# Rounding the token and channel weights to float32 during attention, by way of a DRAM scratch

## The chip, the cores and the metric

The kernel runs on one core of one Trainium2 chip. The metric is the device time of one execution in microseconds. Each kernel is run several times, and the median is compared. Engines are named as in the profile: PE multiplies matrices, PEld loads its stationary operand, DVE is the vector engine, ACT the scalar engine, POOL the GpSimd engine, SP the engine that issues every DMA of this kernel.

## The reference

Three layers follow each other for 4 batches of 768 tokens and 384 channels. First comes a gated linear recurrence over 8 heads of 48 channels ("attention" below). Then comes a layer that mixes tokens by a spatial matrix under a gate. Last come two dense layers over tokens (768 to 256 to 768) and two over channels (384 to 1536 to 384), each pair with a residual:

```python
state = f[:, :, t, :, None] * state + np.einsum('bhd,bhe->bhde', k[:, :, t], v[:, :, t])
y[:, :, t] = np.einsum('bhd,bhde->bhe', q[:, :, t], state)
...
h = np.maximum(x @ w_in, 0.0)                      # u and v are the halves of h
v_s = np.einsum('ts,bsd->btd', w_spatial, v_n) + b_spatial[None, :, None]
x = (u * v_s) @ w_out
...
h = np.maximum(xt @ w_tok1, 0.0) @ w_tok2
u = x + h.transpose(0, 2, 1)
return u + np.maximum(u @ w_ch1, 0.0) @ w_ch2
```

The matrices w_in, w_out, w_tok1, w_tok2, w_ch1 and w_ch2 arrive as float64, w_spatial as float32.

## The kernel before, in words

Every matrix product is done three times: each operand is a sum of a high and a low part (`h` and `l`), and the product of both low parts is left out (`mm3`, lines 126 to 132). So each weight must be split before PE can use it. `split_weight` (line 57) does this in pieces of 128 rows and up to 384 columns. A float64 piece goes through these steps: SP loads it as pairs of 32-bit words (L72). DVE puts the high word's bits in place with two instructions (L78, L81). ACT scales the low word (L85). POOL adds it (L86). ACT squares the high word (L87). DVE sets values to zero that are too small for float32 (L91). These instructions are called the rounding. After it, ACT copies the piece into the high part (L92), and POOL or DVE subtracts to get the low part (L101). A float32 piece needs only a load (L96), the copy and the subtraction. The pool `wst` holds three pieces in flight (`bufs` is 3), with one tile for the loaded words and one, `wsa`, for the result.

The token and channel weights are 34 pieces: w_t1 has 6 pieces of 256 columns, w_t2 has 4, w_c1 12 (8 named wc1, 4 named wc1x) and w_c2 12 of 384 columns.

Work is written down as lists of steps, which `weave` mixes with each other. A scheduler then sets the final order on each engine from these lists. Each engine runs its instructions strictly in that order. In the first phase, for each batch, come the normalised input layer (`s1`: products pv and pu), the token mixing (`mix`: products ps, then DVE L439, ACT L443, DVE L440 and L444) and the output product (`out1`: px, which goes to the DRAM scratch x1d). The attention of the batch after it is woven in; one unit is two heads over half of the tokens. A unit needs on DVE two scans and a product (L204, L211, L214), state updates (L254, L267) and a subtraction (L358). After the third batch's turn there is no attention left to weave in. There the fourth batch's products, the token layers of the first batch (p with wt1, wt2) and the start of the channel layers (p with wc1, po with wc2) are woven with the splitting of the token and channel weights:

```python
        weave(rest + s1(B - 1, 0) + s1(B - 1, 1), staged(st_a + st_b))
...
        m, rest = s23(B - 1)
        weave(m, conv)
...
        weave(c2(0), st_c[:12])
```

This stretch, from about 372 to 520 us, is called the transition below. What follows it is channel layers (L602, L603, L615) for all batches.

Of the kernel before, what the change touches and what calls it, by code (L numbers as in the profile page):

```python
# [18 lines left out]
def tile_kernel(ctx, tc, fkqs, v, w_in, w_sp, b_sp, w_out, w_t1, w_t2, w_c1, w_c2, out):  # L19
    nc = tc.nc  # L20
# [22 lines left out]
    def f32(ap):  # L43
        return ap.bitcast(F32)
# [8 lines left out]

    # weights as sums of two parts of 12 bits each; float64 is rounded to float32 on the way
    LEAST = 3.4332275390625e-05 ** 2

    def split_weight(pool, stage, src, name, n, cols, eng, first=0, order=None):
        """Tiles of both parts, and the steps that fill them, piece by piece."""
        wide = src.dtype == mybir.dt.uint64
        h = pool.tile([P, n, cols], F32R, name=name + "h")  # L60
        l = pool.tile([P, n, cols], F32R, name=name + "l")
        if wide:
            src = src.bitcast(U32)
        srcr = src.rearrange("(n p) c -> n p c", p=P)

        def piece(i, c0, width):
            sl = (slice(None), i, slice(c0, c0 + width))
            at = stage.tile([P, WST], U32, tag="wsa", name=f"{name}sa{i}{c0}")
            a = at[:, :width]
            if wide:  # L70
                st = stage.tile([P, WST, 2], U32, tag="wst", name=f"{name}st{i}{c0}")
                nc.sync.dma_start(  # L72
                    out=st[:, :width, :].rearrange("p c t -> p (c t)"),
                    in_=srcr[first + i][:, 2 * c0 : 2 * (c0 + width)],
                )
                yield
                lo, hi = st[:, :width, 0], st[:, :width, 1]
                nc.vector.tensor_scalar(  # L78
                    out=a, in0=hi, scalar1=3, scalar2=0x3FFFFFFF, op0=ALU.logical_shift_left, op1=ALU.bitwise_and
                )  # L80
                nc.vector.scalar_tensor_tensor(  # L81
                    out=a, in0=hi, scalar=0xC0000000, in1=a, op0=ALU.bitwise_and, op1=ALU.bitwise_or
                )
                # the low word's first 3 bits, rounded
                nc.scalar.activation(lo, lo, AF.Copy, scale=2.0**-29)  # L85
                nc.gpsimd.tensor_tensor(out=a, in0=a, in1=lo, op=ALU.add)  # L86
                nc.scalar.activation(f32(hi), f32(hi), AF.Square)  # L87
                yield
                # zero below float32's least normal number
                a = f32(a)  # L90
                nc.vector.scalar_tensor_tensor(out=a, in0=f32(hi), scalar=LEAST, in1=a, op0=ALU.is_ge, op1=ALU.mult)  # L91
                nc.scalar.copy(h[sl], a)  # L92
                yield
            else:
                a = f32(a)
                nc.sync.dma_start(out=a, in_=srcr[first + i][:, c0 : c0 + width])  # L96
                yield
                nc.scalar.copy(h[sl], a)
                yield
                yield  # L100
            eng.tensor_tensor(out=l[sl], in0=a, in1=f32(h[sl]), op=ALU.subtract)  # L101

        where = [(i, c0, min(WST, cols - c0)) for i in range(n) for c0 in range(0, cols, WST)]
        return h, l, [partial(piece, *x) for x in (order(where) if order else where)]

    def staged(pieces):
        """Steps in which each piece is one stage behind the one after it."""
        gens = []

        def step(n):  # L110
            if n < len(pieces):
                gens.append(pieces[n]())
            for g in gens[max(0, n - 3) : n + 1]:
                next(g, None)

        return [partial(step, n) for n in range(len(pieces) + 3)]

    def weave(main, *fillers):
        """Emit the steps of main with those of the others spread evenly before them."""
        for n, m in enumerate(main):  # L120
            for fl in fillers:
                for x in fl[len(fl) * n // len(main) : len(fl) * (n + 1) // len(main)]:
                    x()
            m()

    def mm3(ps, pairs, first=True, **kw):
        """ps += sum over (lh, ll, rh, rl) of (lh + ll)^T (rh + rl) without the product of both low parts."""
        n = len(pairs)
# [5 lines left out]
    def body(general):  # L134
        # ---------------- phase 1 pools
        x1d = dram.tile([B, S, DM], F32, name=f"x1d{int(general)}")
# [58 lines left out]
        def chunked(u, b, hf, p, fs, fkq, vt):  # L195
            ki, qi = fkq[:, 1, :], fkq[:, 2, :]
            n0 = hf * NCW
            # decay from the chunk's start, and its inverse (from the chunk's end backwards); both scans pass
            # through all chunks and start anew where the factor is zero and the other operand is not
            pg = at2.tile([P, 2, W], F32, tag="pg", name=f"pg{u}")  # L200
# [14 lines left out]
            yield  # L215
            # keys with tokens on partitions
            ncs = NCW if hf == 0 else NCW - 1
# [111 lines left out]
        def att_unit(b, hf, p):  # L329
            """The steps of one pair of heads over half of the tokens."""  # L330
            u = f"{b}{hf}{p}"
# [33 lines left out]
        def att(units):  # L365
            """Steps of these units in turn, the first of each ahead of the unit before it."""
            gens = [att_unit(*x) for x in units]
# [95 lines left out]

        # ---------------- phase 1
        winh, winl, steps = split_weight(
# [10 lines left out]
        out_steps = staged(st_b)  # L476
        rest = []
        for b in range(B - 1):
            if b:
                weave(s1(b, 0), rest)  # L480
            a, rest = s1(b, 1), []
            m, rest = s23(b)
            steps = att(half(b + 1, 0) + half(b + 1, 1))
            cut = len(steps) * len(a) // len(a + m)
            weave(a, steps[:cut], out_steps)
            weave(m, steps[cut:])
            out_steps = []
        right.close()
        wr2 = ExitStack()
        w2p = wr2.enter_context(tc.tile_pool(name="w2p", bufs=1, side="right"))  # L490
        t1h, t1l, st_a = split_weight(w2p, wst, w_t1, "wt1", NCH, DT, nc.gpsimd)
        t2h, t2l, st_b = split_weight(w2p, wst, w_t2, "wt2", NT1, S, nc.gpsimd)
        c1h, c1l, st_c = split_weight(w2p, wst, w_c1, "wc1", NK - 1, DC, nc.gpsimd)
        c1w = [(c1h[:, c, :], c1l[:, c, :]) for c in range(NK - 1)]
# [3 lines left out]
        w2q = wr2.enter_context(tc.tile_pool(name="w2q", bufs=1, side="right"))  # L498
        c1h, c1l, st_c = split_weight(w2q, wst, w_c1, "wc1x", 1, DC, nc.gpsimd, NK - 1)
        c1w.append((c1h[:, 0, :], c1l[:, 0, :]))  # L500
# [8 lines left out]
        if not general:  # L509
            # does any chunk's decay come near float32's range?  # L510
            nc.vector.tensor_reduce(
# [6 lines left out]

        # ---------------- phase 2
        st2 = {}  # L520
# [69 lines left out]
        def ff(b, hf):  # L590
            """Token half hf through both channel layers; a block's second product comes after the next one's first."""
            tsl = slice(hf * W, (hf + 1) * W)
# [59 lines left out]
        otp = e(tc.tile_pool(name="otp", bufs=3))  # L652
        c2h, c2l, st_c = split_weight(w3p, wst, w_c2, "wc2", NF, DM, nc.vector)
        st_c = staged(by_block[2 * NK : 3 * NK] + st_c[:3] + by_block[3 * NK :] + st_c[3:])
# [14 lines left out]
    body(False)  # L669
    # If so, all is done again in a way that holds for any decay.  # L670
    again = nc.values_load(flag, min_val=0, max_val=1)
# [46 lines left out]
```

## Time and profile before

| | |
|---|---|
| median of 3 runs | 834.35 us (833.73 to 834.75) |
| span of the profiled execution, first to last instruction | 835.6 us |
| mean granted TensorE clock of that execution, share of full | 0.976 |
| PE busy, share of the span | 770.3 us, 92% |
| DVE busy | 462.2 us, 55% |
| ACT busy | 277.7 us, 33% |
| POOL busy | 232.9 us, 28% |

The span is the profiled execution's own time; no other time of that execution is given, and the median is that of other executions. Busy shares are means over stages that differ: what a change in one stage is worth has to be read from that stage.

### The profile page before, as it was taken

The numbers are of one execution on the slowest core, as the hardware profiler recorded it, in microseconds if no ns is written. First come the engines' busy times: TensorE is split into PE (matmuls) and PEld (weight loads), VectorE is DVE, ScalarE is ACT, GpSimd is POOL, SyncE is SP. The second block draws the span as 40 slices with busy tenths as digits, with TensorE's granted clock in tenths as the row PEclk, the third lists the DMA queues.
The fourth block names the chain that finished last, engine by engine and source line by source line (L and its number), as shares of the span: only waits on it lengthen the run. The fifth ranks groups of instructions, "written<-read, shape, count | busy, mean of one in ns | idle before, by whom it ended". The sixth has DMA issues, their size and how long they took to land.

```text
span 835.6 us, 12502 instructions
## 1 busy us (share of the span) xinstructions
PE 770.3 (92%) x4785; PEld 708.6 (85%) x4785; DVE 462.2 (55%) x916; ACT 277.7 (33%) x590; POOL 232.9 (28%) x290
## 2 busy tenths in 40 slices
PE   3579599999999999999879889999999999999996
PEld 2357478988889878998769788999999999999995
DVE  6988977783777648638996796222122312222211
ACT  4544543333423343226645553112111311111110
POOL 5786721121112122106873661004001210001000
PEclk9999679999999999999999999999999999999998
DMA  7464321330223211203434321002000200000001
GB/s 248 128 210 131 127 93 56 129 107 33 86 77 110 91 38 57 90 20 107 153 95 130 128 72 59 21 1 86 1 29 1 86 1 28 1 1 30 14 16 34
DMA packets 30055, 61.09 MB, mean 73 GB/s; under 512 B 4128, under 2 KB 19872, under 8 KB 29984
## 3 DMA queue, kind: packets, MB, share of 16 engines
q1 hardware_dynamic: 29984, 60.18, 22.5%
q8 instruction: 40, 0.66, 0.3%
q14 instruction: 31, 0.25, 0.1%
HBM read 48.37 MB, written 9.44 MB: 69 GB/s over the span
## 4 chain that ended last, share of the span: by engine, by line
PE 71%; DVE 15%; DMA 6%; issue 4%; ACT 1%; POOL 1%; SPq 1%; DVEq 0%; ACTq 0%; POOLq 0%
PE po L615 17%; PE p L132 7%; PE p L131 7%; PE p L130 7%; PE ps L130 4%; PE ps L132 3%; PE ps L131 3%; PE pa L229 3%; PE py L285 2%; PE py L279 2%; PE px L130 2%; PE px L132 2%; PE px L131 2%; PE pv L130 2%; PE pu L130 2%
## 5 line engine op out<-in xcount | busy, mean ns | idle before, releaser
L603 DVE SCALAR_TENSOR_TENSOR hl<-p,hh 128x384 fp32r<-128x384 f32 x96 | 53.4, 557 | 176.5 <-ACT hh L602 176.5
L602 ACT ACTIVATE hh<-p 128x384 fp32r<-128x384 f32 x96 | 47.1, 491 | 183.4 <-PE p L132 183.4
L615 PE MATMUL po<-hl,wc2h 128*128 128x384 f32 x288 | 98.2, 341 | 1.4 <-DVE hl L603 1.4
L615 PE MATMUL po<-hh,wc2l 128*128 128x384 f32 x288 | 97.3, 338 | 0.0
L626 POOL TENSOR_TENSOR us<-uh,ul 128x384 f32<-128x384 f32 x24 | 25.4, 1066 | 197.6 <-DVE ul L586 180.3
L615 PE MATMUL po<-hh,wc2h 128*128 128x384 f32 x288 | 76.0, 340 | 4.0 <-ACT hh L602 4.0
L234 POOL TENSOR_SCALAR_AFFINE_SELECT am<-am 128x384 f32<-128x384 f32 x64 | 40.7, 651 | 114.8 <-ACT am L233 114.7
L130 PE MATMUL ps<-wsph,vh 128*128 128x384 f32 x192 | 67.3, 350 | 1.7 <-DVE g L439 1.7
L132 PE MATMUL ps<-wsph,vl 128*128 128x384 f32 x192 | 65.3, 343 | 0.3 <-DVE vl L412 0.3
L131 PE MATMUL ps<-wspl,vh 128*128 128x384 f32 x192 | 65.2, 340 | 0.0
L132 PE MATMUL p<-uh,wc1l 128*128 128x384 f32 x192 | 64.9, 338 | 0.0
L131 PE MATMUL p<-ul,wc1h 128*128 128x384 f32 x192 | 64.7, 337 | 0.0
L130 PE MATMUL p<-uh,wc1h 128*128 128x384 f32 x192 | 64.6, 338 | 0.1
L615 PEld LDWEIGHTS po<-hh,wc2h 128*128 128x128 f32 x288 | 52.4, 189 | 5.5 <-ACT hh L602 5.5
L615 PEld LDWEIGHTS po<-hl,wc2h 128*128 128x128 f32 x288 | 54.5, 189 | 2.7 <-DVE hl L603 2.7
L615 PEld LDWEIGHTS po<-hh,wc2l 128*128 128x128 f32 x288 | 54.5, 189 | 0.0
L279 PE MATMUL py<-fkq,state 112*112 112x128 f32 x160 | 36.1, 324 | 8.1 <-DVE state L254 6.1
L229 PE MATMUL pa<-fkq 48*128 48x128 f32 x384 | 42.5, 331 | 0.9 <-ACT am L233 0.9
L229 PEld LDWEIGHTS pa<-fkq 48*128 48x128 f32 x384 | 31.9, 217 | 10.8 <-issue 5.4
L130 PEld LDWEIGHTS ps<-wsph,vh 128*128 128x128 f32 x192 | 36.2, 188 | 5.0 <-DVE g L439 2.0
L279 PEld LDWEIGHTS py<-fkq,state 112*112 112x112 f32 x160 | 26.7, 198 | 14.9 <-DVE state L254 9.0
L130 PE MATMUL pu<-xh,winh 128*128 128x384 f32 x96 | 34.6, 361 | 5.0 <-ACT u L419 3.4
(167 smaller groups left out, 1933.6 us busy)
## 6 DMA issues: line engine op xcount, KB each, us to landing
fkq<-in_fkq SPq DMA_DIRECT2D x31, 576.0 KB, 3.8
vt<-in_v SPq DMA_DIRECT2D x8, 576.0 KB, 6.0
x1d<-xs SPq DMA_DIRECT2D x24, 192.0 KB, 1.9
xf<-x1d SPq DMA_DIRECT2D x12, 384.0 KB, 4.5
wc2st<-in_w_c SPq DMA_DIRECT2D x12, 384.0 KB, 3.2
out<-ot SPq DMA_DIRECT2D x24, 192.0 KB, 2.0
wc1st<-in_w_c SPq DMA_DIRECT2D x8, 384.0 KB, 3.8
winst<-in_w_in SPq DMA_DIRECT2D x6, 384.0 KB, 4.1
```

The source lines that it names most:

```text
L130: nc.tensor.matmul(ps, lh, rh, start=first and i == 0, stop=False, **kw)
L131: nc.tensor.matmul(ps, lh, rl, start=False, stop=False, **kw)
L132: nc.tensor.matmul(ps, ll, rh, start=False, stop=i == n - 1, **kw)
L229: nc.tensor.matmul(pa[j][:, c, :], ki[64 * j : 64 * j + D, sl], qi[64 * j : 64 * j + D, sl], start=True, stop=True)
L234: nc.gpsimd.affine_select(out=am[j], in_=am[j], compare_op=ALU.is_ge, fill=0.0, base=0, pattern=[[0, NCW], [1, C]], channel_multiplier=-1,)
L279: nc.tensor.matmul(py[:112, c, :], now[c][:112, :112], qi[:112, c * C : (c + 1) * C], start=c == 0, stop=False, skip_group_check=True,)
L285: nc.tensor.matmul(py[64 * j : 64 * j + m, c, :], vt[:, c, h0 + D * j : h0 + D * j + m], am[j][:, c, :], start=False, stop=True, skip_grou ...
L602: nc.scalar.activation(hh, ps, AF.Relu)
L603: nc.vector.scalar_tensor_tensor(out=hl, in0=ps, scalar=0.0, in1=f32(hh), op0=ALU.max, op1=ALU.subtract)
L615: nc.tensor.matmul(po[c], l[:, ft, csl], r, start=ft == 0 and x == 0, stop=ft == NF - 1 and x == 2)
L626: nc.gpsimd.tensor_tensor(out=us[c], in0=f32(uh[:, c, tsl]), in1=f32(ul[:, c, tsl]), op=ALU.add)
```

## The change

The rounding of the four token and channel matrices is taken out of the transition. A new function `round_weight` makes pieces that only round, and write the float32 result to a DRAM scratch (`wt1d`, `wt2d`, `wc1d`, `wc2d`). They are woven in five parts into the first phase of the first three batches. `split_weight` then reads the scratch as a float32 matrix. The rounding instructions stand in a function `rounded`, unchanged in themselves.

```diff
+    def rounded(stage, a, src, c0, width, name):
+        st = stage.tile([P, WST, 2], U32, tag="wst", name=f"{name}st")
+        nc.sync.dma_start(
+            out=st[:, :width, :].rearrange("p c t -> p (c t)"), in_=src[:, 2 * c0 : 2 * (c0 + width)]
+        )
+        yield
...
+        return a
+
+    def round_weight(stage, src, name):
...
+        dst = dram.tile([rows, cols], F32, name=name + "d")
...
+        def piece(i, c0, width):
+            at = stage.tile([P, WST], U32, tag="wsa", name=f"{name}da{i}{c0}")
+            a = yield from rounded(stage, at[:, :width], srcr[i], c0, width, f"{name}d{i}{c0}")
+            nc.sync.dma_start(out=dst[i * P : (i + 1) * P, c0 : c0 + width], in_=a)
...
+                a = yield from rounded(stage, a, srcr[first + i], c0, width, f"{name}{i}{c0}")
                 nc.scalar.copy(h[sl], a)
...
+        early = []
+        if not general:
+            for name, src in (("wt1", w_t1), ("wt2", w_t2), ("wc1", w_c1), ("wc2", w_c2)):
+                kept[name], x = round_weight(wst, src, name)
+                early += x
+            early = staged(early)
+        part = lambda n: early[len(early) * n // 5 : len(early) * (n + 1) // 5]
...
-            weave(a, steps[:cut], out_steps)
-            weave(m, steps[cut:])
-            out_steps = []
+            weave(a, steps[:cut], out_steps if b == 0 else part(2 * b - 1))
+            weave(m, steps[cut:], part(2 * b))
...
-        t1h, t1l, st_a = split_weight(w2p, wst, w_t1, "wt1", NCH, DT, nc.gpsimd)
+        t1h, t1l, st_a = split_weight(w2p, wst, kept["wt1"], "wt1", NCH, DT, nc.gpsimd)
```

The line numbers of the changed kernel are 23 higher in the attention; L65, L68 and L78 are there what L78, L81 and L91 are here.

How the scheduler's order moves is seen first on DVE, in the first batch's turn, ahead of its first mixing (about 128 us in the trace). Before, a unit's scans stood there by themselves (pg is a scan's result, fs and fkq are its inputs):

```order
L202 COPY first<-fs_1297 128x3
L203 MEMSET fs_1297 128x4
L204 SCALAR_TENSOR_TENSOR pg_1299<-fs_1297,first 128x384
L209 TENSOR_SCALAR last<-pg_1299 128x3
L210 RECIPROCAL last<-last 128x3
L211 SCALAR_TENSOR_TENSOR pg_1299<-fs_1297,last 128x384
L254 SCALAR_TENSOR_TENSOR state_124<-z_1034,pend,own 112x2x48
L214 TENSOR_TENSOR fkq_1291<-fkq_1291,pg_1299 128x768
```

In the changed kernel the roundings of wt2 and wc1 stand between the same unit's instructions:

```order
L225 COPY first<-fs_1301 128x3
L277 SCALAR_TENSOR_TENSOR state_125<-z_1242,pend,own 112x2x48
L290 SCALAR_TENSOR_TENSOR z_1245<-z_1242,pend,pk_1231 112x48
L435 TENSOR_TENSOR vl_502<-vf_1080,vh_501 128x512
L226 MEMSET fs_1301 128x4
L65 TENSOR_SCALAR wt2da_2207<-wt2d1384st 128x384
L78 SCALAR_TENSOR_TENSOR wt2da_2147<-wt2d10st,wt2da_2147 128x384
L227 SCALAR_TENSOR_TENSOR pg_1303<-fs_1301,first 128x384
L68 SCALAR_TENSOR_TENSOR wt2da_2207<-wt2d1384st,wt2da_2207 128x384
L277 SCALAR_TENSOR_TENSOR state_124<-z_1038,pend,own 112x2x48
L232 TENSOR_SCALAR last<-pg_1303 128x3
L65 TENSOR_SCALAR wc1da_2254<-wc1d00st 128x384
```

Although the five parts are spread over three batches, all 34 pieces stand in DVE's order behind the first attention units and ahead of the second batch's second mixing. Of the 34, three wt1 pieces stood in this region before as well. By the second batch's first mixing (its L439, at 227.19 us in the trace), DVE has 31 pieces more behind it, and 15 instructions of the attention fewer (one unit's seven from L202 to L214, three L254, one L265, two L267 and two L358).

In the transition, DVE's order before begins so:

```order
L399 BN_STATS bs_4018<-r_4016 128x6
L401 BN_AGGR mv_4020<-bs_4018 128x2
L78 TENSOR_SCALAR wt1sa_4038<-wt1st_4039 128x256
L412 TENSOR_TENSOR vl_3910<-vf_4002,vh_3909 128x512
L81 SCALAR_TENSOR_TENSOR wt1sa_4038<-wt1st_4039,wt1sa_4038 128x256
L78 TENSOR_SCALAR wt1sa_4073<-wt1st_4074 128x256
L399 BN_STATS bs_4053<-r_4051 128x6
```

In the changed kernel it holds the normalisation alone:

```order
L422 BN_STATS bs_4349<-r_4347 128x6
L424 BN_AGGR mv_4351<-bs_4349 128x2
L435 TENSOR_TENSOR vl_4254<-vf_4333,vh_4253 128x512
L422 BN_STATS bs_4377<-r_4375 128x6
L424 BN_AGGR mv_4379<-bs_4377 128x2
```

All roundings are gone from there; what is left of the weights on DVE is the subtraction for wc2 (L124, before L101).

On SP, the loads of the attention's inputs (fkq) stood next to each other in this region:

```order
L338 DMA fkq_1180<-in_fkq 128x1152
L72 DMA wt1st_4039<-in_w_t 128x512
L72 DMA wt1st_4074<-in_w_t 128x512
L72 DMA wt1st_4096<-in_w_t 128x512
L338 DMA fkq_1291<-in_fkq 128x1152
L338 DMA fkq_1420<-in_fkq 128x1152
L338 DMA fkq_1528<-in_fkq 128x1152
```

In the changed kernel loads of float64 pieces and writes to the scratch stand between them:

```order
L361 DMA fkq_1427<-in_fkq 128x1152
L92 DMA wt2d<-wt2da_2207 128x384
L60 DMA wc1d0768st<-in_w_c 128x768
L92 DMA wc1d<-wc1da_2254 128x384
L60 DMA wc1d01152st<-in_w_c 128x768
L92 DMA wc1d<-wc1da_2311 128x384
L60 DMA wc1d10st<-in_w_c 128x768
L92 DMA wc1d<-wc1da_2355 128x384
L60 DMA wc1d1384st<-in_w_c 128x768
L361 DMA fkq_1553<-in_fkq 128x1152
```

A write waits in SP's queue for its piece's last DVE instruction, and what stands behind it waits too.

## Rows read from the trace of the kernel before

**Rows 1.** The page: busy tenths of PE and DVE in 40 slices of 20.9 us.
```profile
PE   3579599999999999999879889999999999999996
...
DVE  6988977783777648638996796222122312222211
```
**Rows 2.** Windows: length, busy time by engine, granted clock, DMA share, GB/s.
```profile
107.00:227.20 120.20, 120.20 (x840) 103.02 (x838) 81.95 (x195) 44.86 (x97) 22.26 (x48) 0.97 0.26 83
227.20:372.00 144.80, 144.80 (x1058) 126.94 (x1057) 94.72 (x228) 48.89 (x108) 25.78 (x49) 1.00 0.22 72
372.00:520.00 148.00, 129.72 (x678) 120.39 (x677) 120.15 (x176) 75.92 (x157) 83.63 (x77) 0.97 0.34 105
```
**Rows 3.** Waits of PE from 372 to 520 us: total, times, longest.
```profile
PE po L615 <- ACT hh L602: 4.0, 4, 1.8
PE pu L130 <- ACT u L419: 3.4, 1, 3.4
PE px L132 <- DVE gl L444: 2.2, 1, 2.2
...
PE pu L130 <- ACT r L397: 1.7, 1, 1.7
PE po L615 <- DVE hl L603: 1.4, 4, 0.6
PE p L131 <- POOL x1l L538: 1.1, 1, 1.1
PE p L575 <- DVE ul L586: 0.5, 1, 0.5
```
**Rows 4.** Waits of all engines there: what ACT waited for.
```profile
ACT wc2st L87 <- DVE wc2sa L81: 7.0, 5, 4.4
```
**Rows 5.** DVE groups from 370 to 525 us: busy us, mean ns.
```profile
L81 DVE SCALAR_TENSOR_TENSOR wc2sa<-wc2st,wc2sa 128x384 uint32<-128x384 uint32 x12 | 11.7, 974 | 0.2
...
L91 DVE SCALAR_TENSOR_TENSOR wc2sa<-wc2st,wc2sa 128x384 f32<-128x384 f32 x12 | 9.9, 829 | 2.5 <-ACT wc2st L87 1.6 <-ACT gh L443 0.9
...
L78 DVE TENSOR_SCALAR wc2sa<-wc2st 128x384 uint32<-128x384 uint32 x12 | 7.6, 636 | 2.1 <-DMA wc2st<-in_w_c 2.0
```
**Rows 6.** Timeline of DVE from 503.7 us, and of POOL there: start, duration.
```profile
503.76 0.55 DVE L81 SCALAR_TENSOR_TENSOR wc2sa<-wc2st,wc2sa 128x384 uint32<-128x384 uint32 x1
504.23 0.35 DVE L78 TENSOR_SCALAR wc2sa<-wc2st 128x384 uint32<-128x384 uint32 x1
504.62 1.27 DVE L81 SCALAR_TENSOR_TENSOR wc2sa<-wc2st,wc2sa 128x384 uint32<-128x384 uint32 x1
505.81 0.35 DVE L78 TENSOR_SCALAR wc2sa<-wc2st 128x384 uint32<-128x384 uint32 x1
506.08 0.55 DVE L603 SCALAR_TENSOR_TENSOR hl<-p,hh 128x384 fp32r<-128x384 f32 x1
...
504.44 1.03 POOL L86 TENSOR_TENSOR wc2sa<-wc2sa,wc2st 128x384 uint32<-128x384 uint32 x1 [5.24 <-DVE wc2sa L81]
```
**Rows 7.** Groups from 492 to 511 us, POOL and then DVE.
```profile
L86 POOL TENSOR_TENSOR wc2sa<-wc2sa,wc2st 128x384 uint32<-128x384 uint32 x6 | 6.5, 1089 | 11.3 <-DVE wc2sa L81 9.0 <-ACT wc2h L92 2.3
...
L101 DVE TENSOR_TENSOR wc2l<-wc2sa,wc2h 128x384 fp32r<-128x384 f32 x7 | 5.3, 760 | 0.1
L91 DVE SCALAR_TENSOR_TENSOR wc2sa<-wc2st,wc2sa 128x384 f32<-128x384 f32 x7 | 4.7, 676 | 0.0
L81 DVE SCALAR_TENSOR_TENSOR wc2sa<-wc2st,wc2sa 128x384 uint32<-128x384 uint32 x5 | 3.5, 695 | 0.1
L603 DVE SCALAR_TENSOR_TENSOR hl<-p,hh 128x384 fp32r<-128x384 f32 x5 | 2.7, 549 | 0.0
L78 DVE TENSOR_SCALAR wc2sa<-wc2st 128x384 uint32<-128x384 uint32 x5 | 2.5, 496 | 2.1 <-DMA wc2st<-in_w_c 2.0
```
**Rows 8.** Window from the last kept wt1 piece to the second batch's first mixing.
```profile
104.27:227.20 122.93, 122.49 (x844) 104.86 (x844) 84.64 (x201) 46.10 (x100) 23.30 (x50) 0.96 0.26 82
```
**Rows 9.** Waits of DVE from 107 to 227.2 us.
```profile
DVE bs L399 <- ACT r L397: 12.3, 3, 9.5
```

More of the change, by code (lines that the diff above doesn't have):

```diff
@@ L55, in tile_kernel @@
     LEAST = 3.4332275390625e-05 ** 2
+    def rounded(stage, a, src, c0, width, name):
[4 more added lines that the diff above has]
+        yield
+        lo, hi = st[:, :width, 0], st[:, :width, 1]
+        nc.vector.tensor_scalar(
+            out=a, in0=hi, scalar1=3, scalar2=0x3FFFFFFF, op0=ALU.logical_shift_left, op1=ALU.bitwise_and
+        )
+        nc.vector.scalar_tensor_tensor(
+            out=a, in0=hi, scalar=0xC0000000, in1=a, op0=ALU.bitwise_and, op1=ALU.bitwise_or
+        )
+        nc.scalar.activation(lo, lo, AF.Copy, scale=2.0**-29)
+        nc.gpsimd.tensor_tensor(out=a, in0=a, in1=lo, op=ALU.add)
+        nc.scalar.activation(f32(hi), f32(hi), AF.Square)
+        yield
+        a = f32(a)
+        nc.vector.scalar_tensor_tensor(out=a, in0=f32(hi), scalar=LEAST, in1=a, op0=ALU.is_ge, op1=ALU.mult)
+        return a
+    def round_weight(stage, src, name):
+        if src.dtype != mybir.dt.uint64:
+            return src, []
+        rows, cols = src.shape
+        dst = dram.tile([rows, cols], F32, name=name + "d")
+        srcr = src.bitcast(U32).rearrange("(n p) c -> n p c", p=P)
+        def piece(i, c0, width):
+            at = stage.tile([P, WST], U32, tag="wsa", name=f"{name}da{i}{c0}")
+            a = yield from rounded(stage, at[:, :width], srcr[i], c0, width, f"{name}d{i}{c0}")
+            nc.sync.dma_start(out=dst[i * P : (i + 1) * P, c0 : c0 + width], in_=a)
+        return dst, [
+            partial(piece, i, c0, min(WST, cols - c0)) for i in range(rows // P) for c0 in range(0, cols, WST)
+        ]
+    kept = {}
     def split_weight(pool, stage, src, name, n, cols, eng, first=0, order=None):
@@ L70, in piece @@
             if wide:
[L71 to L91, printed above, removed]
+                a = yield from rounded(stage, a, srcr[first + i], c0, width, f"{name}{i}{c0}")
                 nc.scalar.copy(h[sl], a)
@@ L490, in body @@
         w2p = wr2.enter_context(tc.tile_pool(name="w2p", bufs=1, side="right"))
-        t1h, t1l, st_a = split_weight(w2p, wst, w_t1, "wt1", NCH, DT, nc.gpsimd)
-        t2h, t2l, st_b = split_weight(w2p, wst, w_t2, "wt2", NT1, S, nc.gpsimd)
-        c1h, c1l, st_c = split_weight(w2p, wst, w_c1, "wc1", NK - 1, DC, nc.gpsimd)
+        t1h, t1l, st_a = split_weight(w2p, wst, kept["wt1"], "wt1", NCH, DT, nc.gpsimd)
+        t2h, t2l, st_b = split_weight(w2p, wst, kept["wt2"], "wt2", NT1, S, nc.gpsimd)
+        c1h, c1l, st_c = split_weight(w2p, wst, kept["wc1"], "wc1", NK - 1, DC, nc.gpsimd)
         c1w = [(c1h[:, c, :], c1l[:, c, :]) for c in range(NK - 1)]
@@ L498, in body @@
         w2q = wr2.enter_context(tc.tile_pool(name="w2q", bufs=1, side="right"))
-        c1h, c1l, st_c = split_weight(w2q, wst, w_c1, "wc1x", 1, DC, nc.gpsimd, NK - 1)
+        c1h, c1l, st_c = split_weight(w2q, wst, kept["wc1"], "wc1x", 1, DC, nc.gpsimd, NK - 1)
         c1w.append((c1h[:, 0, :], c1l[:, 0, :]))
@@ L652, in body @@
         otp = e(tc.tile_pool(name="otp", bufs=3))
-        c2h, c2l, st_c = split_weight(w3p, wst, w_c2, "wc2", NF, DM, nc.vector)
+        c2h, c2l, st_c = split_weight(w3p, wst, kept["wc2"], "wc2", NF, DM, nc.vector)
         st_c = staged(by_block[2 * NK : 3 * NK] + st_c[:3] + by_block[3 * NK :] + st_c[3:])
```

## The prediction, made before the changed kernel ran

> **What bounds the kernel now.** I read four views in order: the page's slices, busy time by windows, PE's waits in one window, and DVE's groups and timeline there. In the slices PE is at 9 or more almost everywhere from the sixth slice on, with a dip about the middle, just where DVE's digits rise to 8 and 9 [rows 1]. So PE is the bound in the attention, and something else in the dip. The windows give its size. From 107 to 372 us PE is busy in every microsecond, while DVE is busy 81.95 of 120.20 us and then 94.72 of 144.80. In the transition, 372 to 520 us, PE is busy 129.72 of 148.00 us, so it idles 18.28 us, and DVE is busy 120.15 us, 81% [rows 2]. The granted clock is 1.00 ahead of the transition and 0.97 in it, which is a part of the time at the lower of the two levels (1.2 instead of 2.4 GHz) after PE had paused; 0.03 of 148 us is 4.4 us of full-clock work. So the transition holds at most 18.28 + 4.4 = 22.7 us that a better order could give back.
>
> PE's waits there name ACT more than DVE: 4.0 us for hh, 3.4 for u, 1.7 for r, and 2.2 and 1.4 us for results of DVE [rows 3]. ACT itself stood in its queue behind squares that waited for the rounding's second DVE instruction, 7.0 us for wc2 alone [rows 4]. So the rounding reaches PE through two queues, DVE's and ACT's.
>
> **What is taken out of the transition.** Of the 34 pieces 31 are rounded there now: 28 of 384 columns and 3 of 256. A wide piece takes on DVE 0.974 + 0.829 + 0.636 = 2.44 us by the means [rows 5]. That gives 28 x 2.44, and two thirds of it for each of the three narrow ones, 73 us out of 120.15. DVE then has about 47 us of work in 148. ACT loses two instructions a piece and POOL one. No engine but PE is then near full, and what remains of PE's idle time is what has no rounding before it. I count as such the waits for gl (2.2), x1l (1.1) and ul (0.5), 3.8 us, and say 4.0. A clock loss goes with idle time in this window as 4.4 to 18.28, or 0.24 us for each us. So the gain is 22.7 - 4.0 x 1.24 = 17.7 us. Its bounds: nothing remains, 22.7; or only the waits go whose releaser is ACT's queue or hl (4.0 + 3.4 + 1.7 + 1.4 = 10.5), 10.5 x 1.24 = 13.0.
>
> The float32 reads that replace the loads are half as long and stand early in SP's order; the high-part copy and the subtraction stay where they were, so they cost nothing new. If that cover went (a read late), the wait next in line would be ACT's copy, and PE's wait for wc2 behind it.
>
> **What is added to the attention.** The order shows that the 31 pieces do not spread over three batches: DVE has all of them between the last kept wt1 piece and the second batch's first mixing, and a few rows behind it. In the trace before, that stretch is 104.27 to 227.20 us: 122.93 us, DVE busy 84.64, PE 122.49 [rows 8]. So DVE has 38.3 us free, of which 12.3 are spent on waiting for r, 9.5 in one go [rows 9]: there DVE is ahead of PE, and may come later at no cost.
>
> The price of a piece on DVE has two ends. With POOL idle, the instruction behind an L81 starts 0.47 us after it and the one behind an L78 0.27 us [rows 6]. With L91 taken as L81, a piece costs 1.21 us; 28 wide ones and 3 at two thirds make 36.3 us. The other part is what POOL's add does to DVE. At 504.44 us POOL starts an add of 1.03 us, and the L81 beside it takes 1.27 us in place of 0.55, while the L603 behind takes 0.55 again [rows 6]. From 492 to 511 us POOL does nothing but six adds. The DVE groups there take 5.3 + 4.7 + 3.5 + 2.5 = 16.0 us, against 7 + 7 + 5 instructions at 0.55 and 5 at 0.35, 12.2 us; L603, which reads PSUM, stays at 0.549 [rows 7]. That is 3.8 us on six adds, 0.63 us an add. With 31 adds it is 19.5 us.
>
> By the order, 15 instructions of the attention now come behind this point; at the window's mean of 84.64 / 201 = 0.42 us [rows 8] they are 6.3 us. DVE thus needs 84.64 + 36.3 - 6.3 = 114.6 us without POOL's toll, 8.3 less than there is, and 134.1 us with it, 11.2 more. I take the second, since most of the attention's DVE instructions read two SBUF tiles as L81 does, not PSUM as L603 does. PE needs as long as before, because its order hardly moves, so it waits those 11.2 us, spread over many short gaps. At the transition's rate of 0.24 the clock takes 2.7 more: 13.9 us. Bounds: 0 us, if POOL's toll falls into waits that DVE has anyway; and 2.44 us a piece, the price in the transition [rows 5], which gives 73 us, 28.4 us too many, 35.2 with the clock. Once DVE is behind, it cannot be made good later: from 227.2 to 372 us PE is full [rows 2].
>
> The Trainium skill, page "SBUF — State Buffer", section "Who interferes with whom", says that a DVE instruction with two SBUF inputs and a GpSimd one that reads SBUF exclude each other, and that the first one holds the shared port pair for its whole length. The trace agrees with L81 at 1.27 us beside an add and L603 at 0.549.
>
> ACT gets 62 instructions, at its mean there of 44.86 / 97 = 0.46 us [rows 2] 29 us on 46.10 in 122.93 us, and POOL 31 adds of 1.09 us, 34 us on 23.30 [rows 7, 8]. Both stay under two thirds, so neither is a bound by itself. SP gets 31 more writes, 31 loads moved to here, and 34 reads. The change puts a wait into SP's queue: each write stands there until its piece's last DVE instruction, and behind it stand the next loads and the attention's fkq. Who waits for that is the next unit's sigmoid on ACT. Three fkq buffers cover it; I charge nothing, and leave it to the slower rival.
>
> **The sum.** Span before 835.6 us. Less 17.7, plus 13.9: 831.8 us. The median of the runs shown, 834.35, is 1.25 us under this span, so the forecast is 830.6, say 831 us: faster by 0.4%. A measurement of this kernel tells about 0.2% (1.7 us) from no change, so this is a narrow verdict.
>
> **The rivals.**
> - *The attention hides all of it.* For it: 38.3 us free on DVE against 36.3 us of instructions, and 9.5 us of it in one place [rows 8, 9]. Against it: POOL's toll, and that DVE's free time is cut into waits of half a us to 2 us. Then only the gain remains: 834.35 - 17.7 = 816.7 us.
> - *DVE becomes the bound of the attention (slower).* The mechanism is the shared queue: each add on POOL halts DVE for its full 1.09 us [rows 7], because a full DVE always has an instruction waiting. 31 adds are then 33.8 us, DVE needs 148.4 in place of 122.93, and PE waits 25.5 us, 31.6 with the clock: 834.35 - 17.7 + 31.6 = 848.3 us. It decides from 14.3 us of waiting on, where gain and loss are equal (17.7 / 1.24); that is (14.3 + 8.3) / 31 = 0.73 us an add. For it: DVE is fuller here than in the transition, where at 81% busy PE already lost 18.28 us [rows 2]. Against it: the add's own toll measured 0.63. The skill's sentence above, taken at its word for every add, is this rival.
> - *The change moves the loss and gains nothing.* If only the 13.0 us go whose releaser is plain, and the attention takes 13.9, the time is 834.35 - 13.0 + 13.9 = 835.3 us, no change that can be measured. For it: wc2's pieces are still read, copied and subtracted in the transition, and x1l stays on POOL.
>
> **How the numbers follow.** Forecast (822 to 832.6 us): 0.45. All hidden (under 822): 0.10. No measurable change (832.7 to 836.0): 0.13. Slower by DVE: 0.32, most of it between 838 and 849. So faster 0.55, same 0.13, slower 0.32. The range for 8 in 10 leaves out one in ten below, which is the case with everything hidden and nothing remaining, and one in ten above: 817 to 846 us. The forecast's own range is 822 to 833.
>
> **What would show each step right or wrong.** In the transition (found by the first norm of the fourth batch to the first plain channel layers) PE's idle time should fall from 18.28 us to about 4, with DVE below 50 us busy there and the clock at 0.99 or 1.00. In the attention DVE should be full, 95% or more, from about 107 us to the second batch's first mixing, and that mixing's L439 should start at about 239 to 241 us in place of 227.19, with PE idle about 11 us on the way and its clock below 1.00. Non-rounding DVE instructions with two SBUF inputs (L211, L440) should be longer there than before. If that mixing comes before 230 us, the first rival is right; after 250 us, the second. If PE still idles over 9 us in the transition, the gain was misread. The prediction is wrong as a whole if PE's new waits come from somewhere else, such as loads held behind the scratch writes on SP.

## The result and the profile after

The changed kernel takes 825.25 us (median of 4 runs, 824.60 to 828.73) against 834.39 us in the same session, a ratio of 0.9897 with a 95% interval of 0.9877 to 0.9917. In a second session it gives 0.9889 (0.9869 to 0.9908). So it is faster by 1.0 to 1.1%, where 0.4% was forecast: the direction was right, the size not.

The profiled execution has a span of 827.0 us, 8.6 us under that of before. Its slices, which answer to [rows 1]:

```profile
PE   3468698999989999999999999999999999999996
...
DVE  6997979989898874864464352122122212222211
...
PEclk9659689999989999999999999999999999999999
```

A slice is 20.7 us. The dip of PE in the middle is gone, and so are DVE's eights and nines there; they now stand further ahead, in the seventh to fourteenth slice, and PE has eights there, in the seventh and the twelfth. By windows (length, busy time of PE, PE loads, DVE, ACT, POOL, granted clock, DMA share, GB/s), first the start, then the stretch up to the second batch's first mixing (L462 here), then two stretches that hold nearly the same work as the second and third line of [rows 2] (their matmul counts differ by 28 and 14):

```profile
0.00:104.30 104.30, 64.27 (x438) 49.09 (x438) 91.00 (x181) 49.72 (x112) 71.20 (x90) 0.74 0.54 169
104.30:245.52 141.22, 127.94 (x820) 107.65 (x816) 128.86 (x280) 70.22 (x155) 68.13 (x79) 0.93 0.59 186
245.52:391.50 145.98, 145.64 (x1086) 127.23 (x1086) 99.41 (x244) 50.37 (x112) 26.02 (x51) 1.00 0.26 82
391.50:515.00 123.50, 122.27 (x692) 119.46 (x691) 53.84 (x86) 47.11 (x98) 45.77 (x46) 1.00 0.27 86
```

The second line answers to [rows 8]: PE idles 141.22 - 127.94 = 13.28 us there, against 0.44 us before. The last line is the transition: PE idles 1.23 us in place of 18.28, at full clock. All that is left of [rows 3] is one wait, from 391.5 to 515 us:

```profile
PE pu L153 <- ACT r L420: 1.2, 1, 1.2
```

A landmark splits the 8.6 us. The third batch's first mixing starts at 322.34 us before and at 341.86 us after; PE has 1,956 matmuls behind it by then in both, the same work.

```profile
341.86 0.55 DVE L462 TENSOR_TENSOR g<-ps,bb 128x384 f32<-128x384 f32 x1
```

So the attention **loses 19.5 us**, and from there to the end the kernel **wins 28.1 us** (513.3 us before, 485.1 after). The second profile gives 17.3 lost and 27.6 won. The forecast had 13.9 and 17.7.

### The profile page after: what moved, and what is told of

Its sections match the earlier page's. It is cut to its first block, busy times and chain, and to the rows that moved or that the text cites. A ratio compares the mean times of both kernels' runs of the same rounds, so it can differ in the third digit from the quotient of the medians.

```text
span 827.0 us, 12669 instructions
## 1 busy us (share of the span) xinstructions
PE 765.1 (93%) x4785; PEld 707.5 (86%) x4785; DVE 443.2 (54%) x916; ACT 274.6 (33%) x590; POOL 240.0 (29%) x290
## 4 chain that ended last, share of the span: by engine, by line
PE 66%; DVE 17%; DMA 6%; issue 5%; POOL 2%; ACT 1%; SPq 1%; DVEq 0%; POOLq 0%; ACTq 0%
PE po L644 18%; PE p L155 8%; PE p L153 8%; PE p L154 8%; PE ps L153 2%; PE ps L155 2%; PE ps L154 2%; PE pa L252 2%; DVE pg L227 2%; PE px L153 2%; PE px L154 2%; PE py L302 2%; PE px L155 2%; PE py L308 1%; DVE state L277 1%
## 5 line engine op out<-in xcount | busy, mean ns | idle before, releaser
L257 POOL TENSOR_SCALAR_AFFINE_SELECT am<-am 128x384 f32<-128x384 f32 x64 | 42.9, 686 | 58.9 <-ACT am L256 58.7
L252 PE MATMUL pa<-fkq 48*128 48x128 f32 x384 | 40.7, 328 | 0.0
L615 DVE TENSOR_TENSOR ul<-p,uh 128x384 fp32r<-128x384 f32 x24 | 13.4, 557 | 47.6 <-ACT uh L614 47.6
```

Source lines behind the costliest of these rows:

```text
L252: nc.tensor.matmul(pa[j][:, c, :], ki[64 * j : 64 * j + D, sl], qi[64 * j : 64 * j + D, sl], start=True, stop=True)
L257: nc.gpsimd.affine_select(out=am[j], in_=am[j], compare_op=ALU.is_ge, fill=0.0, base=0, pattern=[[0, NCW], [1, C]], channel_multiplier=-1,)
L615: nc.vector.tensor_tensor(out=ul[:, c, tsl], in0=ps, in1=f32(uh[:, c, tsl]), op=ALU.subtract)
```

## The experiments

Six sessions on several chips; the kernel before took 832.9 to 836.7 us (medians) in them. So ratios to the kernel before of the same session are compared, and where a ratio is put into us it is taken times 834.4.

**The same kernel again.** No edit.

> The changed kernel unchanged, once more, for a second profile. In the first one PE lost 19.6 us up to the start of the third batch's first mixing (341.9 against 322.3 us) and won 28.2 us from there to the end. Theory (both are the change's): 824 to 826 us, and a split within 2 us of 19.6 and 28.2. Rival (the granted clock of 0.5 between 26 and 63 us in that one execution made much of the 19.6): the loss shrinks to about 14 us, the forecast's, and the gain to about 23.

0.9889; 17.3 lost, 27.6 won. In this profile too the clock was low between 26 and 63 us, so it does not exclude the rival by itself; but the start costs nothing that shows. The first line of the windows above and this one of the kernel before have the same number of matmuls, at a mean clock of 0.74 and 0.93:

```profile
0.00:104.30 104.30, 65.81 (x438) 49.77 (x438) 91.08 (x183) 49.88 (x113) 71.34 (x90) 0.93 0.54 169
```

**Each term by itself.** First the gain:

```diff
-                kept[name], x = round_weight(wst, src, name)
-                early += x
+            flat = v[2:4].rearrange("b s c -> (b s) c")
+            kept["wc2"] = flat
```

and wt1, wt2 and wc1 likewise from v.

> Nothing is rounded in the attention; the transition reads other float32 numbers of the same shapes (from v) in place of the scratch, so this leaves out the rounding of the token and channel weights altogether. It measures the gain term. The forecast's step: 17.7 us, so 816.7 us. The reading of the two traces (idle time under-counts what a pause costs, and all of the clock loss comes back): 26 to 28 us, so 806 to 809 us. If the gain is 22.7 at most, as the windows said, not under 811.5.

0.9664 (0.9645 to 0.9683): 28.0 us. The bound of 22.7 us that the prediction drew from idle time and clock was no bound. Then the loss:

```diff
-                kept[name], x = round_weight(wst, src, name)
+                kept[name], x = src, round_weight(wst, src, name)[1]
```

> The roundings into the scratch stand in the attention as in the change, but the transition reads and rounds the float64 weights as before, so the work is done twice. It measures the loss term. The forecast's step: 13.9 us, so 848.3 us. The reading of the trace after: 18 to 20 us, so 852 to 854 us. If all is hidden: 834.4. If gain and loss are independent, this and the gain alone add up to the changed kernel: their differences from before sum to -9 us.

1.0214 (1.0198 to 1.0229): 17.9 us. The two sum to -10.1 us, the change itself gives -9.3: within 0.8 us, which is less than the intervals, they add up, and both were forecast too small. This kernel's profile has the full clock between 26 and 63 us, and its landmark at 341.09 us, 18.8 us late; so the loss is not the start's clock.

**The early add taken out.**

```diff
-        nc.gpsimd.tensor_tensor(out=a, in0=a, in1=lo, op=ALU.add)
+        if add:
+            nc.gpsimd.tensor_tensor(out=a, in0=a, in1=lo, op=ALU.add)
```

with `add` false for the early pieces.

> The changed kernel without the 34 adds on POOL in the early rounding (so the weights are cut off instead of rounded); DVE's and ACT's instructions, loads and writes stay. Toll theory, the forecast's: DVE then needs 114.6 us of the 122.9 there are, so the loss nearly goes: 806 to 812 us. Rival (the loss comes from DVE's own added instructions, and from the attention's work standing behind them in DVE's queue, not from POOL): 821 to 826 us.

0.9743 (0.9721 to 0.9765), between the two: the adds make 12.2 us of the loss, 6.6 us remain over the gain alone. The window that answers to the second line of the changed kernel:

```profile
104.30:232.99 128.69, 123.96 (x852) 106.04 (x850) 110.75 (x279) 70.43 (x156) 32.82 (x48) 0.96 0.65 204
```

DVE does 279 instructions in 110.75 us, where with the adds 280 take 128.86. That is 18.1 us on 31 adds, 0.58 us an add: the toll was forecast at 0.63. The groups show who pays it, first with the adds, then without (busy us, mean ns):

```profile
L277 DVE SCALAR_TENSOR_TENSOR state<-z,pend,own 112x96 f32<-112x96 f32 x22 | 10.6, 482 | 0.1
...
L430 DVE TENSOR_SCALAR vf<-r,mv,rs 128x512 f32<-128x512 f32 x9 | 9.0, 998 | 1.9 <-POOL rs L428 1.7
...
L225 DVE COPY first<-fs 128x3 f32<-128x3 f32 x9 | 4.6, 508 | 3.3 <-ACT fs L369 3.3
```
```profile
L278 DVE SCALAR_TENSOR_TENSOR state<-z,pend,own 112x96 f32<-112x96 f32 x22 | 7.5, 342 | 0.1
L431 DVE TENSOR_SCALAR vf<-r,mv,rs 128x512 f32<-128x512 f32 x9 | 4.8, 538 | 0.4 <-POOL rs L429 0.3
...
L226 DVE COPY first<-fs 128x3 f32<-128x3 f32 x9 | 1.8, 202 | 6.7 <-ACT fs L370 6.7
```

**The add moved to DVE.** If a full DVE is what PE waits for, it does not matter whether DVE stands still for an add or does it.

```diff
-        nc.gpsimd.tensor_tensor(out=a, in0=a, in1=lo, op=ALU.add)
+        eng.tensor_tensor(out=a, in0=a, in1=lo, op=ALU.add)
```

with `eng` DVE (`nc.vector`) for the early pieces.

> The changed kernel with the early rounding's add moved from POOL to DVE (whose sum of such integers isn't exact, so the weights are a little off). Toll theory: what an add on POOL costs DVE (16 us on 31 adds by DVE's own durations with and without it) is replaced by 31 instructions of 0.55 us, 17 us, so the time stays within 2 us of the changed kernel, a ratio to before of 0.987 to 0.992. Rival (the attention waits because its own work on POOL, the mask of the scores and the norm's rs, queues behind the adds): POOL is free again, and the ratio goes to about 0.975, that of the kernel without the adds.

0.9755 (0.9742 to 0.9769): no dearer than no add at all, as the rival said. The window:

```profile
104.30:237.15 132.85, 127.21 (x870) 109.62 (x871) 121.98 (x308) 70.60 (x154) 32.83 (x49) 0.98 0.61 194
```

DVE is busy 92% of the window, as in the changed kernel (91%), and PE idles 5.6 us in place of 13.3. Against the kernel without adds, DVE has 11.2 us more to do, and the time is the same. So DVE's busy share does not set PE's wait. An excess of DVE's need over the 122.9 us of the forecast is not tested here, since 121.98 us lies just under it; the next run does without any excess.

**The other way round: adds on POOL, nothing on DVE.**

```diff
-        nc.vector.tensor_scalar(
...
-        nc.vector.scalar_tensor_tensor(
...
-        nc.gpsimd.tensor_tensor(out=a, in0=a, in1=lo, op=ALU.add)
+        nc.gpsimd.tensor_tensor(out=a, in0=hi, in1=lo, op=ALU.add)
...
-        nc.vector.scalar_tensor_tensor(out=a, in0=f32(hi), scalar=LEAST, in1=a, op0=ALU.is_ge, op1=ALU.mult)
```

for the early pieces alone; the add then reads the high word as it was loaded.

> The changed kernel without DVE's three instructions of each early piece; load, ACT's two, POOL's add and the write stay (so the scratch holds wrong numbers). It leaves POOL's toll on the attention's own DVE instructions and what queues on POOL. Theory (DVE being full makes the loss): DVE has 20 us or more to spare again, and the loss is under 3 us, a ratio of 0.966 to 0.970. Rival (POOL's queue, or the toll by itself): the loss is 9 us or more, a ratio over 0.977.

0.9858 (0.9841 to 0.9876): 16.2 us over the gain alone, with DVE busy only two thirds of the time. Here the theory that a full DVE makes the loss falls.

```profile
104.30:238.00 133.70, 129.17 (x842) 108.72 (x841) 88.46 (x194) 71.01 (x157) 50.09 (x80) 0.95 0.64 207
```

**Loads, ACT and writes only.** From the kernel just shown:

```diff
-            nc.gpsimd.tensor_tensor(out=a, in0=hi, in1=lo, op=ALU.add)
-            nc.scalar.activation(f32(hi), f32(hi), AF.Square)
+            nc.scalar.activation(f32(a), f32(hi), AF.Square)
```

> The changed kernel with early pieces of a load, two instructions on ACT and a write only (nothing on DVE or POOL, so the scratch holds wrong numbers). If what is left of the loss without adds (8 us) is DVE's own three instructions: no loss, a ratio of 0.965 to 0.969. Rival (loads and writes: SP's queue, in which a write stands before the attention's own loads, or the DMA engines at 0.6 busy in place of 0.3): 0.972 to 0.977.

0.9753 (0.9739 to 0.9767), the same as with DVE's three instructions (0.9743) and with four (0.9755). So DVE's own rounding instructions cost nothing that these runs can tell (their intervals are 1 to 2 us wide either way), and the 7 us that are left without adds are those of loads, ACT and writes.

**How the adds cost.** Two readings were left: DVE instructions of the attention stand still beside an add, or POOL is taken while the attention's mask and the norm's rs stand behind. First an add that waits for its load alone, and whose result nobody reads:

```diff
+        if not add:
+            nc.gpsimd.tensor_tensor(out=aside[:, :width], in0=aside[:, :width], in1=hi, op=ALU.add)
```

> The kernel without the early adds, and beside each early piece an add of the same size on POOL that writes a tile nobody reads and waits for the piece's load alone, not for DVE (the weights are cut off instead of rounded). Theory of the queue (an add that waits at the head of POOL's queue for DVE's second rounding instruction, 35 us in all in the changed kernel, holds the attention's mask and rs behind it): the wait is gone, and the ratio is that without adds, 0.974 to 0.978. Rival (the adds slow DVE while they run, wherever they stand): the ratio stays that of the changed kernel, 0.986 to 0.991.

0.9925 (0.9912 to 0.9939), dearer still. But the wait at the head of POOL's queue is not gone, as the theory wanted: it has become a wait for the loads, 41.0 us in 19 waits up to the second batch's first mixing, where the adds of the changed kernel wait 42.6 us, 34.8 of it for DVE. So this run does not tell the two readings apart. Two lines of the changed kernel:

```profile
POOL wc1da L73 <- DVE wc1da L68: 20.8, 9, 3.6
...
POOL wc2da L73 <- DVE wc2da L68: 7.5, 2, 6.6
```

Then, in the kernel with loads, ACT and writes only, POOL taken by something beside which no DVE instruction grew:

```diff
+            for _ in range(2):
+                nc.gpsimd.tensor_tensor(out=aside, in0=aside, in1=f32(st[:, 0, 1:]), op=ALU.pow)
```

> The kernel whose early pieces are a load, two ACT instructions and a write, with two one-column powers on POOL beside each piece that wait for its load: 1.1 us of POOL's time, as an add takes, in a kind of instruction beside which no DVE instruction was longer in the traces before and after (the scratch holds wrong numbers). Theory of the toll (an add hurts because DVE instructions of the attention stand still beside it): no cost, a ratio of 0.973 to 0.977 as without them. Rival (an add hurts because POOL is taken, and the attention's mask and rs stand behind it): 0.983 to 0.988, as with adds and no DVE work.

0.9708 (0.9685 to 0.9731). Its window stands against that of the kernel with adds only (0.9858, above):

```profile
104.30:231.30 127.00, 123.06 (x833) 103.44 (x831) 80.00 (x194) 69.10 (x154) 65.51 (x111) 0.98 0.68 216
```

POOL is busier here, 65.51 us against 50.09, and the kernel is faster by 1.5%. So POOL's being taken is not by itself what costs. DVE does the same 194 instructions in 80.00 us, 8.5 us less, which fits the toll: the instructions that stand still would be steps of the attention for which PE waits. It does not decide for the toll, because the waits at the head of POOL's queue differ as well: 35.5 us for ACT's scaled word in the kernel with adds only, 19.9 us for the loads here. A run below has such waits and no early add on POOL, and loses as much as the change.

**What loads, ACT and writes cost.** The prediction had left SP's queue at nothing. With the write given out by ACT (`nc.sync.dma_start` becomes `nc.scalar.dma_start` for it):

> The kernel whose early pieces are a load, two ACT instructions and a write, with the write given out by ACT behind its own result instead of by SP (the scratch again holds wrong numbers). Theory (a write at the head of SP's queue, 30 us in all there, keeps the attention's next fkq load back, and the sigmoid waits for it): no wait on SP, a ratio of 0.965 to 0.969. Rival (the traffic itself, or ACT's 62 instructions): 0.973 to 0.977.

0.9737 (0.9721 to 0.9752): SP's waiting writes are not it, to within some 3 us. With no instruction on any engine, loads and writes alone:

```diff
-            nc.scalar.activation(lo, lo, AF.Copy, scale=2.0**-29)
-            nc.scalar.activation(f32(a), f32(hi), AF.Square)
+            a = st.rearrange("p c t -> p (c t)")[:, :width]
```

with st loaded from v.

> The changed kernel with early pieces of a load of as many bytes (of v) and a write of as many as before, and no instruction on any compute engine (the scratch holds numbers of v). Traffic theory (the 6.3 MB read and 6.3 MB written while the attention loads its own, with fkq landing later): the 7 us of the loads, ACT and writes stay, a ratio of 0.972 to 0.977. Rival (ACT's 62 instructions stand in front of the attention's own on ACT): the ratio of the gain alone, 0.964 to 0.968.

0.9893 (0.9871 to 0.9915), far over both expectations. No compute engine paces the pieces now, and what is late is the attention's own input: ACT waits for it from 104.3 to 239.2 us as the first row says, where the kernel before (second row) waited 11.6 us and the changed kernel (third row) 7.5 us on the way to the same mixing.

```profile
ACT fs L374 <- DMA fkq<-in_fkq: 38.3, 10, 5.9
```
```profile
ACT fs L346 <- DMA fkq<-in_fkq: 11.6, 8, 3.6
```
```profile
ACT fs L369 <- DMA fkq<-in_fkq: 7.5, 6, 2.5
```

So this loss is as large as all of the change's, but it is another one, since in the changed kernel the input is not late. Nor is it shown to be the traffic's. Up to the same mixing, the kernel with ACT's two instructions moves as much (second row) and takes 1.4% less:

```profile
104.30:239.20 134.90, 124.42 (x841) 104.69 (x839) 80.45 (x194) 42.31 (x94) 20.80 (x48) 0.98 0.63 201
```
```profile
104.30:231.71 127.41, 124.90 (x837) 105.51 (x833) 79.91 (x194) 69.24 (x156) 24.11 (x48) 0.95 0.63 214
```

A load of fkq lands there in 4.4 us (median) and here in 4.9. What differs more is when SP gives it out: the first one after 110 us at 125.63 us here (first row) and at 117.06 us there, and the six behind it 4 to 7 us later here.

```profile
125.63 0.45 SPq L366 DMA_DIRECT2D fkq<-in_fkq  x1
```
```profile
117.06 0.42 SPq L370 DMA_DIRECT2D fkq<-in_fkq  x1
```

SP waits 51.9 us for transfers to land here and 3.4 us there, with the attention's loads in the same queue. So SP's queue is the nearer reading for this run; no run tells it from the traffic. What makes the 4 to 7 us of the paced kernels (0.9753, 0.9737, 0.9708), traffic or ACT's two instructions, was not told apart either; these three also show that a slightly different order moves the time by some 4 us.

**Versions that keep the gain.** The pieces held back, so that they spread over three batches: a one-column copy on ACT from the newest result into the piece's buffer before its load.

```diff
+        if hold:
+            nc.scalar.copy(f32(st[:, 0, :1]), mark[-1].bitcast(F32))
         nc.sync.dma_start(...)
```

> The changed kernel with its early pieces held to the steps they are written beside: before a piece's load a one-column copy on ACT from the newest norm, gate or mixing result into the piece's buffer, and the pieces dealt out over three batches by time. 31 pieces then stand between about 135 and 370 us instead of 104 and 245. Theory (DVE is filled up only because all pieces are drawn into one stretch; DVE is busy 67% over 104 to 372 us before, and 31 x (1.2 + 0.5) = 53 us more make 87%): the loss falls from 17 to 3 to 7 us, a ratio of 0.970 to 0.976. Rival (each piece costs PE its 0.5 us wherever it stands): the loss and the ratio stay, 0.987 to 0.991.

0.9798 (0.9780 to 0.9816): better than the change by 0.9%, not as good as expected. In its profile PE is full again up to the second batch's first mixing (idle 0.21 us):

```profile
104.30:226.81 122.51, 122.30 (x835) 103.91 (x833) 96.80 (x230) 56.61 (x135) 39.54 (x61) 0.99 0.42 131
```

Held, and with the early add on DVE:

> The held kernel with the early add on DVE as well (again a sum that isn't exact). Theory (what the early rounding costs is PE waiting for steps of the attention that are drawn out, by adds on POOL and by too many pieces in one stretch): both taken away leave a loss of 0 to 3 us, a ratio of 0.966 to 0.970. Rival (the two are one and the same cost, DVE's fullness): 17 us more on DVE undo what spreading gave, and the ratio is 0.976 or more.

0.9749 (0.9731 to 0.9768), between the two expectations: half a per cent better than held alone, no better than the add on DVE alone. The add on DVE with the writes given out by POOL (`nc.gpsimd.dma_start`):

> The changed kernel with the early add on DVE and the scratch writes given out by POOL instead of SP. If SP's queue is the rest of the loss: 0.965 to 0.970, the ratio of the gain alone. Rival (traffic or ACT): 0.973 to 0.977, that of the add on DVE.

0.9883 (0.9864 to 0.9901), against both expectations: it gives back 1.3%. POOL now waits at the head of its queue for the pieces' DVE instructions, 49.6 us in 20 waits up to the second batch's first mixing, and the mask stands behind:

```profile
POOL wc1d L92 <- DVE wc1da L78: 14.2, 4, 5.5
...
POOL wc2d L92 <- DVE wc2da L78: 13.5, 5, 4.2
```

No early add stands on POOL here, and DVE's instructions are nearly as short as without adds (998 ns with them, 538 without, see above):

```profile
L430 DVE TENSOR_SCALAR vf<-r,mv,rs 128x512 f32<-128x512 f32 x9 | 5.2, 579 | 0.4 <-POOL rs L428 0.2
```

Yet the ratio is the changed kernel's (0.9889). So waits at the head of POOL's queue can cost what the adds cost, and how the adds cost, by the toll or by this queue, stays open.

All three together:

> The held kernel with the early add on DVE and the writes given out by POOL: everything that was found to cost is taken away. 0.965 to 0.969 if the rest of the loss is SP's queue; 0.973 to 0.977, the held kernel's with the add on DVE, if it is the traffic, ACT's instructions or the hold itself.

0.9709 (0.9694 to 0.9725): 812.6 us against 836.64 in its session, **24 us under the kernel before** and 15 us under the change, with an add on DVE whose sum the expectations take as not exact; no run here measures by how much. With the pieces spread, writes on POOL do no harm, although POOL waits 82.0 us for them between 104 and 375 us: such waits cost where the pieces stand close together. Against the held kernel with its adds on POOL (0.9798, 52.5 us of such waits) this speaks for a toll as well. 3.8 us over the gain alone remain.

## Why the prediction was right in direction and wrong in size

**The gain (17.7 forecast, 28 measured) was mis-sized, and its stated maximum was wrong.** The step that failed is "the transition holds at most 18.28 + 4.4 = 22.7 us". Three things were missing. First, a pause costs more than its idle time. These rows are from the kernel before (start, duration):

```profile
491.53 0.34 PE L130 MATMUL p<-uh,wc1h 128*128 128x384 f32 x1
491.70 0.34 PE L131 MATMUL p<-ul,wc1h 128*128 128x384 f32 x1
493.26 0.79 PE L615 MATMUL po<-hh,wc2h 128*128 128x384 f32 x3 [1.22 <-ACT hh L602]
```

Matmuls of 0.34 us start every 0.175 us, one inside the other. The next one starts 1.56 us after the last, so 1.385 us are lost where the view says 1.22: the overlap is lost too, 0.165 us. The waits view lists 17 pauses in the transition (13 of them in [rows 3]); at this one's price that is 2.8 us, an estimate. Second, the clock, in windows of 10 us:

```profile
400.00:410.00 10.00, 7.89 (x36) 7.89 (x37) 9.39 (x16) 6.98 (x15) 8.04 (x10) 0.83 0.33 89
430.00:440.00 10.00, 7.30 (x33) 6.16 (x32) 9.97 (x16) 4.91 (x11) 5.74 (x5) 0.89 0.39 120
440.00:450.00 10.00, 10.00 (x56) 9.92 (x55) 8.53 (x13) 5.51 (x12) 5.82 (x6) 0.94 0.61 178
470.00:480.00 10.00, 7.95 (x44) 7.24 (x43) 8.83 (x13) 6.27 (x14) 10.00 (x9) 0.93 0.62 200
480.00:490.00 10.00, 10.00 (x53) 10.00 (x53) 9.97 (x11) 5.18 (x9) 8.69 (x7) 0.90 0.35 116
```

The other windows of the transition are at 1.00; these lack 1.7 + 1.1 + 0.6 + 0.7 + 1.0 = 5.1 us of full clock, and all of it came back: after, the clock is at 1.00 there, with 1.23 us of pauses left. Third, 4.0 us of idle time were kept for waits "that have no rounding before them"; of those (gl, x1l, ul) none is left, so they hung on the roundings too. Idle 17.05 + clock 5.1 + overlap 2.8 = 25.0 us of the 28.1. Of the other 3 us, 1.1 lie behind PE's last matmul (8.1 us to the end before, 7.0 after), a stretch that varies from 6.2 to 8.1 us between the profiles and so need not be the change's; the rest is not located.

**The loss (13.9 forecast, 17.3 to 19.5 measured) was nearer, by a sum whose parts were measured right and whose reason was wrong.** DVE's need was forecast at 114.6 us without the toll and 134.1 with it; 110.75 and 128.86 were measured, and PE's idle time was 13.3 us (11.2 forecast). But the step "PE waits those 11.2 us", by which DVE's need exceeds the window, failed: the adds without DVE's work leave DVE at 88.46 us and still lose 16.2 us, and the loads alone lose 7, as shown. So it was luck that the idle time came near. What PE waits for is the delay of single steps of the attention, and that comes with the adds (9 to 15 us by the pairs of runs; by the toll or by POOL's queue, which was not told apart) and with loads, ACT and writes (4 to 7 us); the instructions on DVE to which the forecast gave 36 us cost nothing that shows. The waits of PE from 104.3 to 245.5 us are spread accordingly, over several releasers:

```profile
PE py L297 <- DVE xl L381: 2.9, 2, 1.9
PE py L297 <- POOL am L257: 2.4, 2, 1.9
PE py L302 <- DVE state L277: 2.1, 5, 0.8
PE pu L153 <- ACT r L420: 1.6, 2, 0.8
PE py L302 <- DVE xl L381: 1.4, 2, 1.0
```

The price of a pause was too low here too: 0.24 us of clock to the us of idle time were charged. By the second line of the windows the clock lacks 7% of 141.22 us, 9.9 us, and by [rows 8] 4% of 122.93 us, 4.9 us, before: 5.0 us where 2.7 were charged. With 12.8 us more idle time that is 17.8 of the 18.3 us by which the second batch's first mixing comes later. In all, the measured loss is 19.5 us on 13.2 us more idle time, 1.48 to 1, and the measured gain 28.1 on 17.05, 1.65 to 1. With these two prices the forecast's own idle times, 14.3 and 11.2 us, give 835.6 - 23.6 + 16.6 = 828.6 us of span, where 827.0 were measured. The prices come from the same profiles, so this is no test of them; it shows that the idle times were forecast well and their price was not.

**Luck.** By the first profile the gain was forecast 10.4 us too small and the loss 5.6 us too small. The two errors have opposite signs and half cancel; that is why 825.25 us still lies in the forecast's own range of 822 to 833 us.

**The other points.** The second batch's first mixing was to start at 239 to 241 us; it started at 245.5 (243.3 in the second profile), between the forecast and the second rival's 250. DVE was to be 95% full; it was 91%. The rival in which all is hidden fell, since the loss alone is 17.9 us; the slower one fell because the toll was 0.58 us an add and not 0.73 or more, and because DVE's fullness is not the mechanism. "I charge nothing" for SP's queue stands for the waiting writes: given out by ACT, they cost as much, and in the changed kernel ACT waits less for fkq than before. Of the instructions named to be longer, L211 and L440 (now L234 and L463) grew little, from 978 and 553 to 1012 and 621 ns; L277 (L254 before), which reads two SBUF tiles too, grew from 333 to 482 ns, and the ones that grew most have one input in SBUF: L430 (L407 before) from 543 to 998 ns, L225 (L202) from 169 to 508. The sentence of the Trainium skill that the prediction cites (page "SBUF — State Buffer", section "Who interferes with whom") stands beside another there, by which copy and tensor_scalar can take the shared pair too, in some modes; the trace agrees with it at L225 and L430, and the prediction had passed over it.

## What to carry to other kernels

Put a price on a pause of the bounding engine from a stretch where it has pauses and one where it has none, not from the idle time alone: here a us of idle time was worth 1.5 to 1.65 us. Filling another engine's free time is not what costs; what costs is a delay put into the steps that the bounding engine waits for, and one instruction on a neighbour (an add on POOL, or a write given out by it) can do that where four on the filled engine do not. An experiment that takes one wait away should be read in its own trace, for the wait may only have changed its reason. Before work is pulled forward, look in the order where it lands: a scheduler draws it into one stretch, and pacing it was worth nearly as much again as the change.

## What was not expected of the hardware

- Two one-column powers on POOL beside a piece's load (a pair took 1.7 to 2.0 us in the costliest cases) left DVE's 194 instructions at 80.00 us; an add of 128x384 in their place, in another run, came with 88.46.
- Loads and writes with no engine work at all cost 19 us (0.9893 against 0.9664), more than the same traffic with ACT's two instructions behind each load (0.9753); the DMA engines were 0.63 busy in both.
- The granted clock stood at 0.50 between 40 and 60 us in some profiles (the third digit of PEclk above) and at full in that of the kernel before, with the same 438 matmuls by 104.3 us: where PE is not the bound, the lower level cost nothing that shows.
